# Zero writes moved into the second to fifth expert, sums scattered earlier, result columns copied by ScalarE

## The chip, the core and the metric

One core of a Trainium2 chip runs the kernel. TensorE (PE, with its weight loads as PEld) does the matmuls, VectorE (DVE) and ScalarE (ACT) read their results, GpSimd (POOL) starts the indirect DMAs (gathers and scatters by a list of row numbers), SyncE (SP) starts the plain ones. Each engine works through its own instructions in order. The time is device microseconds of one launch.

## The reference, cut to what matters

```python
X = np.fft.fft(np.fft.fft(x, axis=1), axis=2).real      # x: 8 x 3072 x 256
x = X.reshape(24576, 256)
# first mixture of 8 experts: all rows, weights P from 8 rounds of Sinkhorn
logits = x @ w_gate;  P = np.exp(logits - logits.max())
for _ in range(8):
    P /= P.sum(1, keepdims=True) + 1e-9
    P /= P.sum(0, keepdims=True) + 1e-9
    P *= N / E
x = sum(P[:, e:e+1] * (np.maximum(x @ w1[e], 0) @ w2[e]) for e in range(E))
# second mixture: each row goes to the expert of its largest logit
e_i = argmax(x @ w_gate2);  g = softmax(x @ w_gate2)[e_i]
out[i] = g * (np.maximum(x[i] @ u1[e_i], 0) @ u2[e_i])
```

`logits.max()` is one maximum over everything, so P is exactly zero for most rows. Their result is zero.

## The kernel before, in words

**Stages.** Transform and logits; `route1`, which lists the rows with a weight above zero; `moe1`, the first mixture on these rows; `route2`, which lists rows by second expert; `moe2`, the second mixture. Everything in `out` that no row reaches has to be written as zero: 49 pieces from a tile `zt`, nearly all of 512 KB, started on SP by `zeros(2)`.

**An expert** (`experts`) takes 3 tiles of 128 rows. The first layer is 8 groups of matmuls (L900, `ph`). After each, ACT takes the relu (`hh`, L886) and DVE the remainder (`hl`, L436), since every product is made of a high and a low half. The second layer is one chain of 24 matmuls for a tile (L933, `py`, of which there are 2 buffers). Besides, five *free* tiles in `moe1` (six in `moe2`) take their weights by gather, one tile an expert from the third on; L946 is their first layer. Weights arrive in one buffer for each half (`rawa`, `rawb`; `rawc` for free tiles); ACT makes the high half (L830) and DVE or POOL the low one (L836, `part`).

**Slots.** All other work is hung on slots (expert, s) by tables of numbers. Slot s is passed after the s-th group of the first layer (0 to 7), within the free tile (8 to 10), at 11, and three times in each tile (12 to 20). `PART` places the weight halves: the last two numbers of a row are those of the free tile's second layer. `ONQ` names the halves that POOL makes. `ZERO` places the zero writes, `SENDS` the scatters; `ask` writes more zeros in the eighth expert, and three more `zeros(2)` stand ahead of `route2`.

**Results of `moe1`.** Sinkhorn runs on DVE beside the experts and ends in slot (5, 8), expert numbers from 0. Until then no result can be weighted, so `keep` copies each to a tile `y` (`YB` = 15 buffers; the next three lie in a buffer of the row pool `Xg`), and later ones are weighted as they are copied. Each slot after (5, 8) then calls `add` once: it multiplies one waiting result by its weight `Rwt` on DVE, copies its 8 columns of second logits to `lg`, and writes it to `acc` in DRAM. A row that has two experts is summed by `send`: an indirect scatter with addition (POOL, L807). Each scatter waits for the one before, and the gathers of `moe2` (L802, `Xg<-acc`) for the last. `spot` builds the matrices that sum the logits of such rows.

**Into `moe2`.** PE runs idle matmuls on zeros (L1282, `warm`) around the matmuls of `route2` (L560). DVE ends the list of row numbers `Rgidx`, POOL gathers six tiles, PE turns the first three (L853), and the first layer (L900) starts.

Of the kernel before, what the change touches and what calls it, by code (L numbers as in the profile page):

```python
# [11 lines left out]
AF = mybir.ActivationFunctionType  # L12
# [1144 lines left out]
def run(tc, ctx, A, out, H, acc, Ld, Pd, Gd, Zd):  # L1157
# [29 lines left out]
    def zeros(n, zt=zt):  # L1187

        t = zat[0]
        if t > 96:  # L1190
            return
        n = min(n, 96 - t) if t < 96 else 1
        if t < 96:
            nc.sync.dma_start(out=out2[t:t + n].rearrange("t p x -> p t x"), in_=zt.to_broadcast([128, n, 512]))
        else:
            nc.sync.dma_start(out=out[24576:24832].rearrange("(p a) d -> p (a d)", a=2), in_=zt[:, 0])
            nc.sync.dma_start(out=out[24832:24960], in_=zt[:, 0, :D])
        zat[0] += n
# [21 lines left out]
    with tc.manual_schedule():  # L1220
# [27 lines left out]
        with ExitStack() as st:  # L1248
# [115 lines left out]
            with ExitStack() as s1:  # L1364
# [12 lines left out]
                def ask():  # L1377

                    for _ in range(5):
                        zeros(2)  # L1380

                turned, more = moe1(nc, K, R, rt, lg, hot, acc, moe, W, part, X, xg, Gd, *rows("w1", "w2"), xb, pt, zeros, zt, later[:2] + (rest, lambda: low(1), grab), ask, rt.C("tro"), lambda i: warm(2), lambda: xg.tile([128, CAP, HW], F32, name="Xg").rearrange("p a b -> p (a b)")[:8, :512])
            with ExitStack() as s1:
# [27 lines left out]

                for _ in range(3):
                    zeros(2)
                later = route2(nc, rt, lg, K, R, r2, ring, arrive, more, Y2, lambda: warm(W3))
# [31 lines left out]
    with tc.If(flag > 0):  # L1446
        with ExitStack() as st:
# [9 lines left out]
}  # L1457
UPART = 6, 11
ONP, ONQ = [], [(7, 5)]
FREE = {"w": (1, 5), "u": 2}  # L1460

BUILD = ((0, (5, 6, 6, 6)), (1, (0, 1, 2, 3)), (2, (1, 2, 3, 4)), (2, (12, 13, 14, 16)), (3, (12, 13, 14, 16)), (5, (0, 1, 2, 3)), (5, (12, 13, 14, 16)))
FBUILD = ((1, (4, 6, 6, 7)), (4, (1, 2, 3, 4)))
ZERO = [(), (), (4, 11, 16), (4, 11, 16), (2, 11, 16), (2, 11, 16), (2, 11, 16), (2,)]
LOGIT = ((0, 11), (0, 11), (0, 13), (0, 20), (1, 5), (1, 12), (1, 18), (2, 2), (0, 16), (2, 7))
# [4 lines left out]
STEPS = [3, 4, 10, 10, 17, 17, 23, 24, 32, 32, 39, 39, 48, 48, 55, 55, 62, 63]  # L1470
FIRST = 1
ADDS, SENDS = tuple(range(21)), {5: (14, 19), 6: (3, 8, 12, 16), 7: (1,)}

# [119 lines left out]
def moe1(nc, K, R, rt, lg, hot, acc, moe, W, part, X, xg, Gd, w1f, w2f, xb, pt, zeros, zt, rest, ask, trash, warm, grow):  # L1593
# [49 lines left out]
    def keep(t, p):  # L1643
        n = late["n"] = late.get("n", -1) + 1
        if YB <= n < YB + CAP:
            if n == YB:
                late["x"] = xg.tile([128, CAP, HW], F32, name="Xg")
            y = late["x"][:, n - YB, :DW]
        else:
            y = late["y"].tile([128, DW], F32, name="y")  # L1650
        if t < E * CAP and not alone(t):
            G.memset(y[:, DG:], 0.0)
        else:
            nc.scalar.activation(out=y[:, DG:], in_=R["ow"][:, t:t + 1], func=AF.Copy)
        nc.scalar.activation(out=y[:, :DG], in_=p, func=AF.Copy, **({"scale": R["wt"][:, t:t + 1]} if known[0] else {}))  # L1655
        ys.append((t, y, p if known[0] else None))

    def add():

        if ys:  # L1660
            t, y, k = ys.pop(next((i for i, v in enumerate(ys) if v[0] >= E * CAP), 0))
            if k is None:
                o.ts(y[:, :DG], y[:, :DG], R["wt"][:, t:t + 1], ALU.mult)
            if t // CAP != E - 1:
                o.cp(lg[:, t], y[:, D:DG])
                if t < E * CAP and not alone(t):
                    spot(t // CAP)
                    hot[-1][2]()
            if t < E * CAP:
# [14 lines left out]
    def send():  # L1684
        if sq:
            a, i, y = sq.pop(0)
            sent.append(a)
            scatter(nc, a, i, y, compute_op=ALU.add)

    def spot(e):  # L1690

# [9 lines left out]

        hot.append((r, m, moved))

    def begin():
# [26 lines left out]
    for i, k in enumerate(steps):  # L1731
        sl.at(*pl[k], lambda i=i: late["sink"][i]())
    sl.at(*pl[steps[-1]], lambda: known.__setitem__(0, True), *[add] * FIRST)
    for e, s in pl[steps[-1] + 1:]:
        if s in ADDS and (e, s) < (E - 1, 6):
            sl.at(e, s, add)

    for e, at in SENDS.items():
        for s in at:
            sl.at(e, s, send)  # L1740
# [121 lines left out]
```

## Time and profile before

| | us |
|---|---|
| median of 3 runs | 662.18 (656.67 to 663.15) |
| profiled execution | 660.44, span 658.7 |
| PE busy | 627.1 (95% of the span) |
| DVE, ACT, POOL busy | 442.6, 321.6, 194.6 |

Stages in the span: transform to 196 us, `route1` to 246, `moe1` to 445 with `route2` from 432 on in its shadow, `moe2` from 466. The profile names a line, an engine, an operation and out<-in; "[4.75 <-DMA x]" is idle time of that engine before the instruction and what ended it.

### The profile page before, as it was taken

The page shows a single profiled execution, that of the slowest core. Times are in us where ns is not written, and L with a number is a line of the kernel's source. Part 1 is how long each engine was busy: PE and PEld are TensorE (multiplying, and loading weights), DVE is VectorE, ACT ScalarE, POOL GpSimd, SP SyncE. Part 2 cuts the span into 40 slices and gives each one's busy share as a digit, 9 for nine tenths or more (in the row PEclk, how much of TensorE's full clock was granted, in tenths as well). Part 3 has the DMA queues.
Part 4 walks back from the last instruction along what each step waited for, and adds up shares of the span by engine and source line. Part 5 has one row for each costly group of instructions (what it writes and reads, how often), then busy time and mean ns, then how long its engine had stood idle before and what let it go on. Part 6 is the DMA issues. An engine that isn't in the chain of part 4 may idle for free. (4 is left out here: it accounts for less than half of the span.)

```text
span 658.7 us, 12655 instructions
## 1 busy us (share of the span) xinstructions
PE 627.1 (95%) x4794; PEld 600.1 (91%) x4794; DVE 442.6 (67%) x1019; ACT 321.6 (49%) x717; POOL 194.6 (30%) x325
## 2 busy tenths in 40 slices
PE   9999999999998989999999998997999999999985
PEld 6899999999998968999999988984899999999984
DVE  4697787777238948659898789664555664674570
ACT  3455555555544204657556555531455564574441
POOL 0002221022110078831201102123686654431331
PEclk9999999999999879999999999998899999999988
DMA  8999999999979765676766758992565547635500
GB/s 222 285 234 323 279 274 280 260 301 308 343 256 374 300 192 177 199 269 206 258 206 218 281 179 229 307 374 44 176 214 194 205 148 296 237 138 210 208 33 29
DMA packets 56785, 152.58 MB, mean 232 GB/s; under 512 B 8292, under 2 KB 25836, under 8 KB 49165
## 3 DMA queue, kind: packets, MB, share of 16 engines
q1 hardware_dynamic: 47500, 114.69, 54.4%
q0 software_dynamic: 8752, 36.50, 17.0%
q8 instruction: 40, 0.66, 0.4%
q10 hardware_dynamic: 464, 0.51, 0.2%
q14 instruction: 29, 0.23, 0.1%
HBM read 101.50 MB, written 50.07 MB: 230 GB/s over the span
## 5 line engine op out<-in xcount | busy, mean ns | idle before, releaser
L933 PE MATMUL py<-w2h,hh 128*128 128x256 f32 (+1 forms) x472 | 137.0, 290 | 1.4 <-ACT y L1655 1.4
L436 DVE SCALAR_TENSOR_TENSOR hl<-ph,hh 128x384 fp32r<-128x384 f32 (+1 forms) x161 | 84.6, 542 | 78.1 <-ACT hh L886 75.8
L933 PE MATMUL py<-w2l,hh 128*128 128x256 f32 (+1 forms) x472 | 134.5, 285 | 2.3 <-DVE w2l L836 2.0
L933 PE MATMUL py<-w2h,hl 128*128 128x256 f32 (+1 forms) x472 | 134.9, 286 | 1.3 <-DVE hl L436 1.0
L886 ACT ACTIVATE hh<-ph 128x384 fp32r<-128x384 f32 (+1 forms) x161 | 75.8, 481 | 60.4 <-PE ph L900 32.7
L933 PEld LDWEIGHTS py<-w2l,hh 128*128 128x128 f32 x472 | 90.3, 191 | 2.7 <-DVE w2l L836 2.2
L933 PEld LDWEIGHTS py<-w2h,hl 128*128 128x128 f32 x472 | 90.1, 191 | 2.1 <-DVE hl L436 1.6
L933 PEld LDWEIGHTS py<-w2h,hh 128*128 128x128 f32 x472 | 90.1, 191 | 1.8 <-ACT y L1655 1.6
L900 PE MATMUL ph<-xh,w1h 128*128 128x384 f32 x256 | 68.2, 348 | 4.3 <-DVE hl L436 3.8
L900 PE MATMUL ph<-xh,w1l 128*128 128x384 f32 x256 | 65.3, 336 | 0.0
L900 PE MATMUL ph<-xl,w1h 128*128 128x384 f32 x256 | 65.3, 336 | 0.0
L74 PE MATMUL pp<-ca,w 96*128 96x96 f32 x512 | 59.0, 275 | 0.0
L74 PEld LDWEIGHTS pp<-ca,w 96*128 96x128 f32 x512 | 58.2, 192 | 0.5 <-ACT Z L97 0.2
L807 POOL DMA_INDIRECT out_dram<-y,Rorow x30 | 31.8, 1062 | 89.5 <-ACT hh L886 37.8
L126 POOL TENSOR_TENSOR lc<-hd 128x32 f32<-128x32 f32 (+1 forms) x25 | 9.5, 380 | 164.4 <-ACT hd L122 149.4
L900 PEld LDWEIGHTS ph<-xh,w1h 128*128 128x128 f32 x256 | 45.0, 189 | 7.6 <-DVE hl L436 6.0
L84 DVE COPY t<-pp 128x512 f32<-128x512 f32 (+2 forms) x56 | 33.3, 608 | 24.2 <-PE pp L82 24.2
L91 PE MATMUL pp<-cb,t 128*128 128x128 f32 x368 | 47.5, 276 | 0.6 <-DVE t L84 0.6
L900 PEld LDWEIGHTS ph<-xh,w1l 128*128 128x128 f32 x256 | 46.5, 189 | 0.0
L900 PEld LDWEIGHTS ph<-xl,w1h 128*128 128x128 f32 x256 | 46.3, 188 | 0.0
L76 ACT ACTIVATE at<-pp 128x384 f32<-128x384 f32 x64 | 31.1, 491 | 30.6 <-PE pp L74 30.1
L91 PEld LDWEIGHTS pp<-cb,t 128*128 128x128 f32 x368 | 44.4, 192 | 0.9 <-DVE t L84 0.8
(346 smaller groups left out, 1262.9 us busy)
## 6 DMA issues: line engine op xcount, KB each, us to landing
out_dram<-zt SPq DMA_DIRECT2D x48, 512.0 KB
H<-hd SPq DMA_DIRECT2D x24, 562.0 KB
xa<-in_xa_dram SPq DMA_DIRECT2D x32, 384.0 KB
xm<-in_xm_dram SPq DMA_DIRECT2D x32, 384.0 KB
rawa<-in_w_dram SPq DMA_DIRECT2D x8, 1024.0 KB
rawb<-in_w_dram SPq DMA_DIRECT2D x8, 1024.0 KB
rawa<-in_u_dram SPq DMA_DIRECT2D x8, 1024.0 KB
rawb<-in_u_dram SPq DMA_DIRECT2D x8, 1024.0 KB
```

The lines of the kernel that those rows point to most:

```text
L74: nc.tensor.matmul(p[:M, i], lhs(4 * h + i), ca, start=True, stop=True)
L76: nc.scalar.activation(out=at[:M, :, :, s0:s0 + 4], in_=p[:M].rearrange("m s g j -> m g j s"), func=AF.Copy)
L84: nc.vector.tensor_copy(out=t[:, :n, :M], in_=p[:, :n, :M])
L91: nc.tensor.matmul(p[:M, i * 128:(i + 1) * 128], t[:, i, :M], cb[:, (g0 + i) * 128:(g0 + i + 1) * 128], start=True, stop=True)
L126: nc.gpsimd.tensor_tensor(out=lc[:np_, :n], in0=hd[:np_, :, 129:137], in1=hd[:np_, :, 273:281], op=ALU.add)
L436: self.nc.vector.scalar_tensor_tensor(out, a, s, b, op0, op1)
L807: nc.gpsimd.indirect_dma_start(out=dst, out_offset=bass.IndirectOffsetOnAxis(ap=idx, axis=0), in_=src, in_offset=None, **kw)
L886: self.nc.scalar.activation(out=a[:, :n], in_=p[:, :n], func=AF.Relu)
L900: self.nc.tensor.matmul(p[:, :N], w, xx, start=(i == 0), stop=(i == 5))
L933: self.nc.tensor.matmul(p[:, :nd], c, W[2 + m // 4][w][:, m % 4, :nd], start=(m == 0 and i == 0), stop=(m == 7 and i == 2))
```

## The change

- Zero writes: `ZERO` now has 2, 6, 6, 6, 2 and 1 in the second to seventh expert (before: 3 in each of the third to seventh, 1 in the eighth). `ask` makes one instead of five, and the three ahead of `route2` are gone. There are as many in all.
- Waiting results may take a second `Xg` buffer: six instead of three lie there (`YB` to `YB + 2 * CAP`, `CAP` = 3).
- `keep` copies the logits' columns on ACT from PSUM. `know`, in slot (5, 8), multiplies those of waiting results by their weights in two DVE instructions. `add` no longer copies them.
- `add` weights a result that no scatter uses (`alone`) on ACT, the others on DVE. Slot (5, 8) makes 3 additions (`FIRST`) instead of 1.
- `SENDS`: seven scatters in the sixth and seventh expert, none placed in the eighth.
- `spot` for experts 1 to 6 stands in slots (6, 12) to (6, 19) and no longer in `add`.
- `moe2`, last expert: the free tile's halves stand in slots 7 and 12 instead of 0 and 2, and DVE makes both, POOL none.

```diff
-                    for _ in range(5):
-                        zeros(2)
+                    zeros(2)
...
-                for _ in range(3):
-                    zeros(2)
                 later = route2(nc, rt, lg, K, R, r2, ring, arrive, more, Y2, lambda: warm(W3))
...
-          (3, 6, 7, 13, 0, 2), (3, 5, 7, 13, 0, 2), (3, 5, 7, 13, 0, 2), (2, 5, 7, 13, 0, 2)],
+          (3, 6, 7, 13, 0, 2), (3, 5, 7, 13, 0, 2), (3, 5, 7, 13, 0, 2), (2, 5, 7, 13, 7, 12)],
-ONP, ONQ = [], [(7, 5)]
+ONP, ONQ = [], []
-ZERO = [(), (), (4, 11, 16), (4, 11, 16), (2, 11, 16), (2, 11, 16), (2, 11, 16), (2,)]
+ZERO = [(), (16, 19), (9, 11, 13, 15, 17, 19), (9, 11, 13, 15, 17, 19), (9, 11, 13, 15, 17, 19), (2, 5), (2,), ()]
-FIRST = 1
-ADDS, SENDS = tuple(range(21)), {5: (14, 19), 6: (3, 8, 12, 16), 7: (1,)}
+FIRST = 3
+SPOTS = (6, 12), (6, 13), (6, 15), (6, 16), (6, 18), (6, 19)
+ADDS, SENDS = tuple(range(21)), {5: (14, 18), 6: (1, 5, 9, 13, 18)}
...
-        if YB <= n < YB + CAP:
-            if n == YB:
+        if YB <= n < YB + 2 * CAP:
+            if (n - YB) % CAP == 0:
                 late["x"] = xg.tile([128, CAP, HW], F32, name="Xg")
-            y = late["x"][:, n - YB, :DW]
+            y = late["x"][:, (n - YB) % CAP, :DW]
...
-        nc.scalar.activation(out=y[:, :DG], in_=p, func=AF.Copy, **({"scale": R["wt"][:, t:t + 1]} if known[0] else {}))
+        by = {"scale": R["wt"][:, t:t + 1]} if known[0] else {}
+        nc.scalar.activation(out=y[:, :DG], in_=p, func=AF.Copy, **by)
+        if t // CAP != E - 1:
+            nc.scalar.activation(out=lg[:, t], in_=p[:, D:DG], func=AF.Copy, **by)
...
             if k is None:
-                o.ts(y[:, :DG], y[:, :DG], R["wt"][:, t:t + 1], ALU.mult)
-            if t // CAP != E - 1:
-                o.cp(lg[:, t], y[:, D:DG])
-                if t < E * CAP and not alone(t):
-                    spot(t // CAP)
-                    hot[-1][2]()
+                if alone(t):
+                    nc.scalar.activation(out=y[:, :DG], in_=y[:, :DG], func=AF.Copy, scale=R["wt"][:, t:t + 1])
+                else:
+                    o.ts(y[:, :DG], y[:, :DG], R["wt"][:, t:t + 1], ALU.mult)
...
+    def know():
+        known[0] = True
+        for a in (0, E * CAP):
+            n = sum(a <= t < a + E * CAP for t, *_ in ys)
+            v = lg[:, a:a + n]
+            o.tt(v, v, R["wt"][:, a:a + n, None].to_broadcast([128, n, 8]), ALU.mult)
...
-    sl.at(*pl[steps[-1]], lambda: known.__setitem__(0, True), *[add] * FIRST)
+    sl.at(*pl[steps[-1]], know, *[add] * FIRST)
...
+    for e, (i, k) in enumerate(SPOTS):
+        sl.at(i, k, lambda e=e + 1: spot(e))
```

Three places show how instructions move. On SP, from the eighth expert of `moe1` to the start of `moe2` (`acc<-y` a result's direct write, `rawa`, `rawb` the weights of `moe2`), before:

```order
L1217 DMA rawa<-in_u_dram 128x2048
L1672 DMA acc<-y 128x264
L1194 DMA out_dram<-zt 128x2x512
L1672 DMA acc<-y 128x265
L1217 DMA rawb<-in_u_dram 128x2048
L1672 DMA acc<-y 128x265
L1194 DMA out_dram<-zt 128x2x512 x6
L1217 DMA rawa<-in_u_dram 128x2048
L1194 DMA out_dram<-zt 128x2x512 x2
L1196 DMA out_dram<-zt 128x512
L1197 DMA out_dram<-zt 128x256
```

and in the change:

```order
L1217 DMA rawa<-in_u_dram 128x2048
L1671 DMA acc<-y 128x264
L1671 DMA acc<-y 128x265
L1217 DMA rawb<-in_u_dram 128x2048
L1671 DMA acc<-y 128x265
L1196 DMA out_dram<-zt 128x512
L1197 DMA out_dram<-zt 128x256
L1217 DMA rawa<-in_u_dram 128x2048
```

Nine writes of 512 KB have left this stretch. On ACT, in the sixth expert of `moe1` where the weights `Rwt` become known, before:

```order
L830 ACTIVATE w1h<-rawa 128x1024
L1654 ACTIVATE y<-Row 128x1
L1655 ACTIVATE y<-py,Rwt 128x264
L856 ACTIVATE xh<-pt 128x384 x2
L1616 ACTIVATE Xg<-Xg,Rsg 128x127 x3
L830 ACTIVATE w1h<-rawa 128x1024
L1655 ACTIVATE y<-py,Rwt 128x264
```

and in the change:

```order
L830 ACTIVATE w1h<-rawa 128x1024
L1665 ACTIVATE y<-y,Rwt 128x264 x2
L1652 ACTIVATE Xg<-Row 128x1
L1654 ACTIVATE Xg<-py,Rwt 128x264
L1656 ACTIVATE lg<-py,Rwt 128x8
L856 ACTIVATE xh<-pt 128x384 x2
L1665 ACTIVATE y<-y,Rwt 128x264
L1614 ACTIVATE Xg<-Xg,Rsg 128x127 x3
L830 ACTIVATE w1h<-rawa 128x1024
L1665 ACTIVATE y<-y,Rwt 128x264
L1654 ACTIVATE Xg<-py,Rwt 128x264
L1656 ACTIVATE lg<-py,Rwt 128x8
```

The free tile's result goes to `Xg`, and four weightings and two column copies stand ahead of or between the next ones. On DVE, in the last expert of `moe2` (`w2l<-rawb` the expert's own low halves, `w2l<-rawc` those of its free tile), before:

```order
L836 TENSOR_TENSOR w2l<-rawc,w2h 128x4x256
L436 SCALAR_TENSOR_TENSOR hl<-ph,hh 128x384 x2
L836 TENSOR_TENSOR w2l<-rawb,w2h 128x4x256
L436 SCALAR_TENSOR_TENSOR hl<-ph,hh 128x384 x3
L439 CAST Rorow<-Xg 128x3
L442 TENSOR_REDUCE s_7767<-Xg 128x3
L427 TENSOR_TENSOR e_7766<-Xg,s_7767 128x24
L836 TENSOR_TENSOR w2l<-rawb,w2h 128x4x256
L436 SCALAR_TENSOR_TENSOR hl<-ph,hh 128x384 x2
```

and in the change:

```order
L836 TENSOR_TENSOR w2l<-rawb,w2h 128x4x256
L436 SCALAR_TENSOR_TENSOR hl<-ph,hh 128x384 x2
L442 TENSOR_REDUCE s_7759<-e_7758 128x3
L431 TENSOR_SCALAR s_7759<-s_7759 128x3
L1800 RECIPROCAL Rpw<-s_7759 128x3
L836 TENSOR_TENSOR w2l<-rawc,w2h 128x4x256
L436 SCALAR_TENSOR_TENSOR hl<-ph,hh 128x384
L836 TENSOR_TENSOR w2l<-rawc,w2h 128x4x256
```

The expert's own second half (first row here) now has no `rawc` half ahead of it; the free tile's two follow the last `hl`. POOL's `w2l<-rawc` is gone.

## Rows read from the trace of the kernel before

**Rows 1.** Waits of PE: for what, us in total, times, longest.
```profile
PE pt L853 <- DMA Xg<-acc,Rgidx: 4.7, 1, 4.7
```

**Rows 2.** Timeline of PE, sixth to seventh expert: start, us, instruction, idle before.
```profile
387.94 0.39 PE L933 MATMUL py<-w2h,hh 128*128 128x264 f32 x1 [1.44 <-ACT y L1655]
...
393.91 3.73 PE L946 MATMUL ph<-Xg,fw 128*128 128x128 f32 x32
...
400.37 0.62 PE L900 MATMUL ph<-xh,w1h 128*128 128x384 f32 x2 [1.68 <-DVE hl L436]
```

**Rows 3.** Timeline of ACT there.
```profile
387.31 0.20 ACT L1654 ACTIVATE y<-Row 128x1 f32<-128x1 f32 x1 [5.97 <-DMA acc<-y]
387.43 0.46 ACT L1655 ACTIVATE y<-py,Rwt 128x264 f32<-128x264 f32 x1
387.79 0.86 ACT L856 ACTIVATE xh<-pt 128x384 fp32r<-128x384 f32 x2
...
390.35 0.47 ACT L1655 ACTIVATE y<-py,Rwt 128x264 f32<-128x264 f32 x1
```

**Rows 4.** Timeline of DVE, from the weights to the list of rows.
```profile
384.88 0.20 DVE L436 SCALAR_TENSOR_TENSOR Rwt<-P 128x24 f32<-128x24 f32 x1
...
399.76 1.81 DVE L436 SCALAR_TENSOR_TENSOR hl<-ph,hh 128x384 fp32r<-128x384 f32 x4
...
452.41 0.19 DVE L427 TENSOR_TENSOR Rgidx<-pt,d 128x30 int32<-128x30 f32 x1
```

**Rows 5.** Groups by line, DVE: out<-in xcount | busy us, mean ns | idle before.
```profile
L431 DVE TENSOR_SCALAR y<-y,Rwt 128x264 f32<-128x264 f32 x15 | 5.3, 352 | 0.0
```

**Rows 6.** Timeline of POOL: first and last of eight scatters, then gathers of `moe2`.
```profile
399.85 1.62 POOL L807 DMA_INDIRECT acc<-y,Rapos  x1 [11.52 <-DMA out_dram<-zt]
...
453.49 1.69 POOL L807 DMA_INDIRECT acc<-y,Rapos  x1 [2.94 <-issue]
458.37 1.02 POOL L802 DMA_INDIRECT Xg<-acc,Rgidx  x1 [3.19 <-issue]
459.69 0.98 POOL L802 DMA_INDIRECT Xg<-acc,Rgidx  x1 [0.30 <-issue]
```

**Rows 7.** Timeline of PE into `moe2`.
```profile
451.75 4.89 PE L1282 MATMUL py<-zb 128*128 128x512 bf16 x14
461.39 0.66 PE L853 MATMUL pt<-ident,Xg 128*128 128x128 f32 x2 [4.75 <-DMA Xg<-acc,Rgidx]
...
466.13 0.70 PE L900 MATMUL ph<-xh,w1h 128*128 128x384 f32 x2
```

**Rows 8.** Windows: us, busy of PE, PEld, DVE, ACT, POOL, clock, DMA share, GB/s.
```profile
260.00:380.00 120.00, 115.77 (x835) 113.48 (x836) 97.30 (x244) 70.04 (x169) 34.33 (x53) 0.99 0.69 227
410.00:445.00 35.00, 34.78 (x248) 32.12 (x248) 24.16 (x66) 15.28 (x29) 6.54 (x5) 1.00 1.00 328
456.00:456.50 0.50, 0.50 (x3) 0.10 (x1) 0.00 (x0) 0.00 (x0) 0.00 (x0) 1.00 0.82 72
461.00:466.00 5.00, 4.61 (x14) 2.52 (x15) 0.19 (x1) 0.71 (x2) 3.76 (x4) 0.50 0.40 109
636.00:640.00 4.00, 3.35 (x16) 3.35 (x17) 2.40 (x7) 0.47 (x1) 0.00 (x0) 0.59 0.00 0
```

**Rows 9.** Timelines of DVE, POOL and PE, last expert of `moe2`.
```profile
628.11 1.23 DVE L836 TENSOR_TENSOR w2l<-rawb,w2h 128x1024 fp32r<-128x1024 f32 x1
...
632.53 4.07 DVE L836 TENSOR_TENSOR w2l<-rawb,w2h 128x1024 fp32r<-128x1024 f32 x1 [1.24 <-ACT w2h L830]
...
633.12 2.38 POOL L836 TENSOR_TENSOR w2l<-rawc,w2h 128x1024 fp32r<-128x1024 f32 x1
...
636.65 0.52 PE L933 MATMUL py<-w2l,hh 128*128 128x256 f32 x1 [2.05 <-DVE w2l L836]
```

**Rows 10.** Timelines of SP and ACT: a weight load's start and its first reader.
```profile
338.67 0.35 SPq L1217 DMA_DIRECT2D rawa<-in_w_dram  x1
...
353.76 1.05 ACT L830 ACTIVATE w1h<-rawa 128x1024 fp32r<-128x1024 f32 x1
```

More of the change, by code (lines that the diff above doesn't have):

```diff
@@ L1702, in spot @@
         hot.append((r, m, moved))
+        if e < E - 1:
+            moved()
     def begin():
```

## The prediction, made before the changed kernel was run

> **What bounds the kernel now.** I read the page first: PE is busy 627.1 of 658.7 us, and its clock is at full speed in nearly all slices. So the time is PE's own work plus the few places where it stands still or runs at the low clock, and a change pays only there. The waits of PE are the second view. Their largest single piece is the gather into the second mixture, 4.7 us [rows 1]. I then put every wait on PE's timeline and asked which of them touches something that the diff moves. Four do: 1.44 us in the sixth expert of `moe1`, where a chain finds no free `py` buffer; 1.68 us in the next, where DVE is late with `hl` [rows 2]; 4.75 us ahead of the first transposes of `moe2` [rows 7]; 2.05 us in the last expert of `moe2` [rows 9]. The rest lies in the transform, `route1` and Sinkhorn and is left as it is. Last, I followed each of the four back through ACT, DVE, POOL and the DMAs.
>
> **A, the sixth and seventh expert.** ACT stands 5.97 us for a free `y` buffer, until a result has been written to `acc` at 387.31 [rows 3]. With three more places in `Xg` this result needs no buffer. It needs `Rwt`, which DVE ends at 384.88 + 0.20 = 385.08 [rows 4], and ACT now has two weightings ahead of it. No row has ACT weighting 264 columns in SBUF; the copy of 264 columns from PSUM takes 387.79 - 387.43 = 0.36 us until the next instruction starts [rows 3], and I take that. The small copies take about 0.1 (387.43 - 387.31). So ACT has let go of the `py` buffer at 385.08 + 2 x 0.36 + 0.1 + 0.36 + 0.1 = 386.4. PE came to that point at 387.94 - 1.44 = 386.5: the wait goes.
>
> It does not go for good. Before, the next result is read from 390.35 to 390.82, 2.56 us after `xh` began (387.79) [rows 3]. In the change `xh` begins at 386.4, and between it and that result stand two more weightings: 386.4 + 2.56 + 2 x 0.36 + 0.36 + 0.1 = 390.1. PE's tile, begun at 386.5, takes (393.91 - 387.94) / 2 = 2.98 us [rows 2], so PE is there at 389.5 and waits 0.6. Of 1.44 us some 0.8 is kept; I count 0.6, since ACT is now full there.
>
> The 1.68 us at 400.37 came from DVE, which began the relu remainders of the free tile only at 399.76, four in a row [rows 4]. Between 385.08 and there the change takes six of twelve weightings from DVE, 6 x 0.35 = 2.1 us [rows 5], and thirteen column copies and two `spot` pieces besides, and adds two short multiplications. The weightings alone are more than the 1.68; the wait goes. The `spot` pieces go to the tiles of the seventh expert, where DVE has room: it is busy 24.16 of 35 us there [rows 8]. A is 0.6 + 1.7 = 2.3 us; the ends are 0 and 3.1.
>
> **B, into `moe2`.** The scatters form a chain, 399.85 to 453.49, and the first gather starts at 458.37, when the last scatter has landed 4.9 us after its start [rows 6]. The list of rows was ready at 452.41 + 0.19 = 452.6 [rows 4]. In the quiet after 445 the chain's step is these 4.9 us; over all seven steps it is (453.49 - 399.85) / 7 = 7.7, beside zero writes that hold the DMA engines at a share of 1.00 from 410 to 445 [rows 8]. In the change these writes are gone, and the first scatter may start in slot (5, 14), with the eighth addition, before PE ends that expert at 393.91 [rows 2]. Seven scatters of 4.9 us are then done at about 428. The eighth needs the first tile of the last expert, two tiles of 2.98 us before `moe1` ends at 445, so 439 and a copy, and lands by 445. So the gather waits for the list alone: start 452.8 instead of 458.37. The first transposes followed it by 461.39 - 458.37 = 3.0 us [rows 6, 7], which gives 455.8. PE's idle matmuls last to 456.64 [rows 7] and become the bound. Gathers 1.32 us apart [rows 6] bring the third at 458.4; ACT's `xh` takes 0.9, and the first layer starts near 459.5 instead of 466.13 [rows 7]. That is 6.6 us: 4.75 of waiting and 1.9 of clock. For the clock I rely on one row: it is full at 456.0 to 456.5, before PE fell idle, and at the low level (0.50) from 461 to 466, after it stood [rows 8]. With PE at work throughout, it should stay up. If it stays at 0.50, the three rounds take 5 us as before (461.39 to 466.13), and B is 4.75. Ends: 4.4 and 7.2.
>
> **C, the last expert of `moe2`.** The low half that PE waits for takes DVE 4.07 us instead of 1.23, and the one other thing of note is that POOL makes a half of the same size from 633.12 for 2.38 us [rows 9]. With POOL's half gone and DVE's at 1.23 it is ready at 632.53 + 1.23 = 633.8. PE came to it at 636.65 - 2.05 = 634.6: no wait. After the wait the clock was at its low level, 0.59 over 636 to 640 [rows 8], and without it about 1.8 us of matmuls at half speed come back. C is 2.05 + 1.8 = 3.85. The two halves of the free tile now come in slots 7 and 12, some 2 us before its chain, which stands behind a tile and 20 matmuls of L946. All later results and scatters shift with PE. Ends: 0, if the half is late for another reason, and 3.9.
>
> The pages know that case. By the Trainium skill, SBUF — State Buffer, section "SBUF: two separate sides", a DVE instruction with two inputs in SBUF and a GpSimd instruction that reads SBUF lock each other out for a whole instruction. The trace agrees: POOL ended at 635.50, 1.23 us more make 636.73, and DVE ended at 636.60, though its start stands before POOL's. By that rule the 2.05 us go with POOL's instruction, and the low end of C is unlikely.
>
> **D, what is added elsewhere.** 23 column copies of 0.1 us on ACT stand in stretches where it is busy 70.04 of 120 us [rows 8]. Eleven more zero writes, 5.8 MB, fall into 260 to 380, where the DMA engines move 227 GB/s at a share of 0.69 [rows 8]. At the 328 GB/s of the full stretch they need 18 us of 120, which there is. A weight load starts 15.1 us before its first reader [rows 10]; behind three zero writes it lands (1.5 + 1.0) MB / 328 GB/s = 8 us after its start. Both are hidden; I count 0.5 us against the change, ends 0 and 3.
>
> **Sum.** 2.3 + 6.6 + 3.85 - 0.5 = 12.25. From the profiled 660.44 that gives 648.2. This execution lies 1.7 us under the median of the runs, 662.18; half of that added, I predict 649.0. From the low ends, 0 + 4.4 + 0 - 3, the gain is 1.4, and from the high ends 14.2. I don't expect the low ends together.
>
> **Rivals.**
> 1. *ACT becomes the bound* in the sixth and seventh expert. Eleven weightings and the copies stand in its queue ahead of relus. For: in A it is already the one waited for. Against: it is busy 70 of 120 us in the experts before [rows 8], so it has room to catch up. Price: A lost and 2 us more; 660.44 - 8.0 + 0.5 = 652.9. Chance 0.14.
> 2. *The gather still waits* for something that I put early: the last scatter, or a direct write of the last results, which ACT starts only after its part in `route2`. For: a wait for several semaphores is told by the last alone. Against: the last scatter has 7 us of room. B is then lost, and 660.44 - 2.3 - 3.85 + 0.5 = 654.8. Chance 0.10.
> 3. *The end gains nothing*, since DVE began the half only when ACT's `w2h` was there, at 632.53 [rows 9], and ACT may be as late for another reason. 660.44 - 8.9 + 0.5 = 652.0. Chance 0.09.
> 4. *Slower: the zero writes hold up weights* in the third to fifth expert, the fetch of `rawa` standing behind three on SP's queue and the gathers of the free tile's weights beside them. It decides once a load needs over 15.1 us [rows 10], that is 1.8 times my 8. To lose all of the gain and 1% more, about 19 us, three experts must each wait 6, with loads landing after 21 us. For: the scatters' step grew from 4.9 to 7.7 us beside such writes. Against: there is no long wait for any weight load in `moe1` now, and the share has 0.3 to give. Time about 667. Chance 0.05.
>  Beside this stands a rule: the Trainium skill, DMA: Bandwidth & Descriptors, section "Issuing engines are not separate DMA queues", says that transfers started by SP, ACT and POOL share the same 16 engines and interleave. By it the gathers slow down in these experts as the scatters did at the end. It is why rival 4 has a chance at all.
>
> **How the numbers follow.** The forecast, all three parts within 2 us of their sizes, has 0.62: 645 to 652. With rivals 1 and 3 at 652 to 653 that makes 0.85; their own spread and some of rival 2 take the upper end to 655. Range 644.5 to 655. About 1% is what a measurement of this kernel can tell from no change: 655.6 and 668.8 around 662.18. Faster: the forecast and rivals 1 and 3 whole, rival 2 mostly on its near side: 0.88. Slower takes rival 4's upper half and an unseen cause, 0.04; within 1% the rest, 0.08.
>
> **What the profile of the changed kernel would show.** A: no wait of ACT for `acc<-y` in the sixth expert, a short PE wait for ACT's result copy, none for `hl` after it. B: the first gather within 0.5 us of `Rgidx`; the last scatter at least 5 us before it; the wait before the transposes under 0.5 us, and the clock at full speed in them. C: every `w2l` on DVE near 1.2 us, no wait before the last expert's tile, the clock full to the last tile. D: no new wait for `rawa`, `rawb`, `fw`. The prediction is wrong if the gather is released by a DMA again, if PE waits for relus in the seventh expert, or if PE's waits between 260 and 380 grow by more than 1 us.

## The result, and the profile after

The changed kernel took **651.51 us** (median of 4 runs, 651.31 to 652.38), the kernel before 662.05 us (4 runs, 656.67 to 663.15). The ratio is 0.9887, with a 95% interval of 0.9851 to 0.9922: 1.1% faster. The forecast was 649.0, with a range of 644.5 to 655.0. The profiled execution took 651.56 us at a span of 649.8.

The waits of PE in the changed kernel (for what, us in total, times, longest):

```profile
PE ph L900 <- DVE hl L436: 4.9, 5, 2.7
...
PE py L933 <- ACT lg L1656: 0.9, 2, 0.7
...
PE pt L853 <- DMA Xg<-acc,Rgidx: 0.2, 1, 0.2
```

The gather that cost 4.7 us [rows 1] costs 0.2. ACT's small copies have become a wait, as expected, and the longest single wait is now one of 2.7 us for `hl` that was not foreseen. PE's timeline says where, in `moe1` (start, us, instruction, idle before); it answers to [rows 2]. The first line is the kernel before, the others the changed one:

```profile
297.50 0.61 PE L900 MATMUL ph<-xh,w1h 128*128 128x384 f32 x2 [0.44 <-DVE hl L436]
```

```profile
301.51 0.62 PE L900 MATMUL ph<-xh,w1h 128*128 128x384 f32 x2 [2.75 <-DVE hl L436]
...
390.75 0.39 PE L933 MATMUL py<-w2h,hh 128*128 128x264 f32 x1 [0.21 <-ACT lg L1656]
...
394.66 0.39 PE L933 MATMUL py<-w2h,hh 128*128 128x264 f32 x1 [0.73 <-ACT lg L1656]
```

The waits of 1.44 and 1.68 us in the sixth and seventh expert are gone, 0.21 and 0.73 have come. The wait for `hl` in the third expert was 0.44 us in the kernel before and is 2.75 now. ACT there, answering to [rows 3]; no wait for a write to `acc` is left:

```profile
389.16 0.92 ACT L1665 ACTIVATE y<-y,Rwt 128x264 f32<-128x264 f32 x2 [3.78 <-DVE Rwt L436]
...
390.08 0.46 ACT L1654 ACTIVATE Xg<-py,Rwt 128x264 f32<-128x264 f32 x1
390.44 0.25 ACT L1656 ACTIVATE lg<-py,Rwt 128x8 f32<-128x8 f32 x1
```

Into `moe2`, POOL (first and last scatter, gathers) and PE, answering to [rows 6] and [rows 7]; DVE had the list of rows at 454.12 + 0.19:

```profile
398.25 1.62 POOL L807 DMA_INDIRECT acc<-y,Rapos  x1 [20.05 <-DVE y L431]
...
445.28 1.56 POOL L807 DMA_INDIRECT acc<-y,Rapos  x1 [3.29 <-ACT y L1654]
454.58 1.75 POOL L802 DMA_INDIRECT Xg<-acc,Rgidx  x1 [7.74 <-DVE Rgidx L427]
456.64 0.98 POOL L802 DMA_INDIRECT Xg<-acc,Rgidx  x1 [0.30 <-issue]
```

```profile
453.46 4.89 PE L1282 MATMUL py<-zb 128*128 128x512 bf16 x14
458.36 0.43 PE L853 MATMUL pt<-ident,Xg 128*128 128x128 f32 x2
...
461.65 0.83 PE L900 MATMUL ph<-xh,w1h 128*128 128x384 f32 x2
```

The last scatter starts 9 us ahead of the gather, and the gather follows the list by 0.27 us. The transposes begin when the idle matmuls end in this execution. Windows (us, busy of PE, PEld, DVE, ACT, POOL, clock, DMA share, GB/s), answering to [rows 8]:

```profile
260.00:380.00 120.00, 113.40 (x831) 110.48 (x829) 96.34 (x247) 70.23 (x184) 41.31 (x63) 1.00 0.80 269
410.00:445.00 35.00, 34.75 (x248) 32.09 (x248) 25.10 (x65) 17.29 (x36) 8.27 (x7) 1.00 0.70 175
454.00:457.00 3.00, 3.00 (x8) 1.03 (x7) 1.41 (x3) 0.00 (x0) 2.11 (x2) 0.50 0.00 0
457.00:462.00 5.00, 4.77 (x22) 1.98 (x20) 0.37 (x1) 0.87 (x2) 3.78 (x5) 0.99 0.42 109
636.00:640.00 4.00, 4.00 (x36) 4.00 (x35) 0.00 (x0) 0.93 (x2) 0.96 (x1) 1.00 0.12 39
```

The zero writes have moved: 269 instead of 227 GB/s over 260 to 380, 175 instead of 328 over 410 to 445. The clock is full in the transposes and in the last expert; 0.50 is the lower of its two levels, 1.2 of 2.4 GHz, and a value between is the mean of a stretch that holds both. DVE's halves there, answering to [rows 9], all take 1.2 us:

```profile
628.05 1.23 DVE L836 TENSOR_TENSOR w2l<-rawb,w2h 128x1024 fp32r<-128x1024 f32 x1 [1.24 <-ACT w2h L830]
...
630.63 1.21 DVE L836 TENSOR_TENSOR w2l<-rawc,w2h 128x1024 fp32r<-128x1024 f32 x1
...
632.23 1.21 DVE L836 TENSOR_TENSOR w2l<-rawc,w2h 128x1024 fp32r<-128x1024 f32 x1
```

**Where the time came from.** To compare runs I cut each profile at four of PE's instructions: the wait for `cs` in the third expert of `moe1` (mark M, 311.97 before, 315.97 after), the last L933 of `moe1` (445.03, 446.74), the first L900 of `moe2` (466.13, 461.65) and the last matmul (650.23, 642.01). "A" is the stretch from M to the end of `moe1`, "B" from there into `moe2`, "C" from there to the last matmul, each from start to start. The last four columns tell of the part ahead: when the wait for L112's operand ends (late in the transform), the clock granted in 10 to 20, 40 to 60 and 260 to 265 us, and the wait for `hl` in the third expert.

```
profile                      A       B       C     L112   clock, three stretches   wait
before                    133.06   21.10   184.10  187.22   1.00 1.00 0.66         0.44
changed                   130.77   14.91   180.36  192.50   0.84 0.83 1.00         2.75
e1 end only               132.81   20.31   180.19  190.29   1.00 0.83 1.00         1.40
e2 zeros only             133.02   14.88   181.95  192.69   0.86 0.83 1.00         2.32
e3 zeros back             130.69   21.56   180.76  190.51   1.00 0.83 1.00         0.54
e4 no early zeros         130.69   14.88   180.19  192.91   0.88 0.83 1.00         1.16
e5 half on POOL           130.71   15.75   180.69  188.08   1.00 1.00 0.66         0.44
e6 old slots              130.68   14.95   181.41  192.74   0.86 0.83 1.00         0.44
e7 short room             132.54   14.95   180.20  187.03   1.00 1.00 0.66         0.44
e8 weightings on DVE      129.20   14.94   180.37  190.16   1.00 0.83 0.94         0.43
e9 both                   129.22   14.94   180.31  192.13   0.83 0.83 1.00         0.56
e10 changed again         130.65   14.92   180.88  192.48   0.84 0.83 1.00         3.02
```

A gave 2.29 us, B 6.19, C 3.74, together 12.22. What follows the start of the last matmul is 0.7 shorter. Against this M comes 4.00 us later: 12.2 + 0.7 - 4.0 = 8.9, the difference of the two spans. The experiments ask what made A, B and C, and what those 4.00 us are.

### The profile page after: what moved, and what is told of

The parts are those of the page before. It is cut to its first block, busy times and chain, and to the rows that moved or that the text cites. A ratio compares the mean times of both kernels' runs of the same rounds, so it can differ in the third digit from the quotient of the medians.

```text
span 649.8 us, 12657 instructions
## 1 busy us (share of the span) xinstructions
PE 627.6 (97%) x4794; PEld 602.0 (93%) x4794; DVE 435.7 (67%) x985; ACT 328.8 (51%) x754; POOL 196.2 (30%) x324
## 5 line engine op out<-in xcount | busy, mean ns | idle before, releaser
L933 PE MATMUL py<-w2h,hh 128*128 128x256 f32 (+1 forms) x472 | 136.0, 288 | 0.9 <-ACT lg L1656 0.9
L933 PE MATMUL py<-w2h,hl 128*128 128x256 f32 (+1 forms) x472 | 133.6, 283 | 1.3 <-DVE hl L436 1.3
L933 PE MATMUL py<-w2l,hh 128*128 128x256 f32 (+1 forms) x472 | 133.1, 282 | 0.3 <-DVE w2l L838 0.3
L933 PEld LDWEIGHTS py<-w2h,hl 128*128 128x128 f32 x472 | 88.8, 188 | 2.1 <-DVE hl L436 2.1
L933 PEld LDWEIGHTS py<-w2h,hh 128*128 128x128 f32 x472 | 89.0, 188 | 1.5 <-ACT lg L1656 1.4
L933 PEld LDWEIGHTS py<-w2l,hh 128*128 128x128 f32 x472 | 89.0, 189 | 0.5 <-DVE w2l L838 0.5
L900 PE MATMUL ph<-xh,w1h 128*128 128x384 f32 x256 | 67.9, 346 | 5.0 <-DVE hl L436 4.9
L900 PE MATMUL ph<-xl,w1h 128*128 128x384 f32 x256 | 65.3, 337 | 0.0
L900 PE MATMUL ph<-xh,w1l 128*128 128x384 f32 x256 | 65.2, 336 | 0.0
L74 PE MATMUL pp<-ca,w 96*128 96x96 f32 x512 | 61.8, 283 | 0.0
L74 PEld LDWEIGHTS pp<-ca,w 96*128 96x128 f32 x512 | 61.0, 199 | 0.8 <-issue 0.3
L807 POOL DMA_INDIRECT out_dram<-y,Rorow x30 | 33.2, 1107 | 86.2 <-ACT hh L886 45.9
L900 PEld LDWEIGHTS ph<-xh,w1h 128*128 128x128 f32 x256 | 44.8, 188 | 8.3 <-DVE hl L436 7.0
L900 PEld LDWEIGHTS ph<-xl,w1h 128*128 128x128 f32 x256 | 46.3, 188 | 0.1
L900 PEld LDWEIGHTS ph<-xh,w1l 128*128 128x128 f32 x256 | 46.3, 188 | 0.0
```

Of the source, the lines that this page charges most:

```text
L74: nc.tensor.matmul(p[:M, i], lhs(4 * h + i), ca, start=True, stop=True)
L807: nc.gpsimd.indirect_dma_start(out=dst, out_offset=bass.IndirectOffsetOnAxis(ap=idx, axis=0), in_=src, in_offset=None, **kw)
L900: self.nc.tensor.matmul(p[:, :N], w, xx, start=(i == 0), stop=(i == 5))
L933: self.nc.tensor.matmul(p[:, :nd], c, W[2 + m // 4][w][:, m % 4, :nd], start=(m == 0 and i == 0), stop=(m == 7 and i == 2))
```

## Experiments

In the experiments, e1 to e4 ran on one chip (kernel before: 657.4 us, median of 25 runs, 654.25 to 661.49), e5 to e8 once each (before 657.0), e9 and e10 side by side (before 659.26, 11 runs, 657.14 to 661.84). The runs of one kernel lie up to 7 us apart, those of e3 11, so I read the stages, and take the times second. Each kernel has one profile (the changed one two). Where nothing was changed in a stage it mostly repeats within 0.3 us. B moves by 0.8 where PE stalls long ahead of the transposes (before and e1) and in e5, C by up to 0.7 (in e10 by a wait of 0.55 for `fw` near 547, where 0.3 had been expected at most; e6 has the same wait), and in e2, whose end is that of the kernel before, C is 2.2 shorter than there; e2 and e5 are told below.

**What made B: e2 and e3.** One has the zero writes moved and nothing else, the other everything but that.

```diff
 e2, in the kernel before
-                    for _ in range(5):
-                        zeros(2)
+                    zeros(2)
...
-                for _ in range(3):
-                    zeros(2)
...
-ZERO = [(), (), (4, 11, 16), (4, 11, 16), (2, 11, 16), (2, 11, 16), (2, 11, 16), (2,)]
+ZERO = [(), (16, 19), (9, 11, 13, 15, 17, 19), (9, 11, 13, 15, 17, 19), (9, 11, 13, 15, 17, 19), (2, 5), (2,), ()]
 e3, in the changed kernel: the same three pieces the other way round
```

Expected of e2: 

> The kernel before with the zero writes alone moved to the second to sixth expert. If the zero writes were what made the scatters slow, the step falls from 7.7 us towards 4.9, the last scatter lands before the list of rows is there, the gather starts within 0.5 us of the list, and B comes nearly whole (5 to 6.6 us) although the scatters are sent from their old slots: 656 to 657, less up to 2.3 us if the new wait of 2.75 us in the third expert comes with it (then 658 to 659). If the earlier slots and the nine rooms are what counts, the gather still waits 3 us or more behind the last scatter: 660 or more. The waits of 1.44 and 1.68 us in the sixth and seventh expert stay.

Expected of e3: 

> The changed kernel with the zero writes where they were before. If they slow the scatters, eight scatters 7.7 us apart from 398 on end at 452 and land at 457, so that the gather waits 3 to 5 us for the last one: 655 to 657. If the earlier and denser sending is enough, the gather starts with the list and the time is that of the changed kernel, 651.5. If the zero writes of the second expert make the wait of 2.75 us in the third, that wait is gone here (back to 0.4) and either figure is 2.3 us less.

Measured: e2 654.75 us (10 runs, ratio to before 0.9933, 0.9904 to 0.9963), e3 654.38 us (10 runs, 646.10 to 657.12; ratio 0.9922, 0.9880 to 0.9964, from the seven under 656). By the medians e2 gains only 2.7 us; its profile reaches M at 315.56, 3.2 us after e1's, so the time doesn't show the stage whole. In e2, with the old scatter slots, B is 14.88, all of the gain. In e3, with the new ones, it is 21.56, none of it. The gather of e2 starts 1.0 us behind the list and not within the 0.5 expected, but it ends 2.0 us behind it, as the changed kernel's does. The gather and PE's wait in e3:

```profile
451.62 1.56 POOL L807 DMA_INDIRECT acc<-y,Rapos  x1 [3.02 <-issue]
456.18 1.02 POOL L802 DMA_INDIRECT Xg<-acc,Rgidx  x1 [2.99 <-issue]
```

```profile
459.13 0.66 PE L853 MATMUL pt<-ident,Xg 128*128 128x128 f32 x2 [6.84 <-DMA Xg<-acc,Rgidx]
```

The list was there at 449.94; the gather waited 6.2 us longer, until the last scatter had landed 4.6 us after its start. The eight scatters were 7.85 us apart on average, beside 305 GB/s at a DMA share of 0.94 from 410 to 445; in the changed kernel 6.72, beside 175 at 0.70. So **the zero writes alone made B**. With them gone the first L900 comes 7.3 to 7.4 us after the list of rows in each of e2, e4, e9 and the changed kernel: the list and the gathers behind it are the bound now, and the scatters' earlier slots buy nothing.

**What made C: e1, e5 and e6.**

```diff
 e1, in the kernel before
-(2, 5, 7, 13, 0, 2)]          last row of the table for "u"
+(2, 5, 7, 13, 7, 12)]
-ONP, ONQ = [], [(7, 5)]
+ONP, ONQ = [], []
 e5, in the changed kernel: ONQ = [(7, 5)] again, slots 7 and 12 kept
 e6, in the changed kernel: slots 0 and 2 again, ONQ empty
```

Expected of e1: 

> The kernel before with the end change alone: the half on GpSimd goes to VectorE, and the two halves of the free tile's `w2` come in slots 7 and 12 of the last expert. By the prediction's C: no `w2l` half on VectorE above 1.3 us, no wait of TensorE before the last expert's tile, clock full to the end, and 3.4 to 3.9 us off the kernel before: 658.4 where the median is 662.05. Rival 3, the half is late for another reason: the wait of about 2 us stands and the time is 661 to 662. Between them, wait gone but clock low: 660.

Expected of e5: 

> The changed kernel with one `w2l` half of the last expert on GpSimd again, the slots 7 and 12 kept. From the first L900 of `moe2` to TensorE's last matmul the kernel before takes 184.1 us, the changed one 180.4. If the two engines hinder each other, one VectorE instruction beside GpSimd's takes over 2 us again, and the stage is 181.5 to 184; if the slots 7 and 12 start the half early enough, VectorE's longer instruction is hidden and the stage stays at 180.4 to 180.8. If the slots alone were the cause, every VectorE half stays at 1.2 us.

Expected of e6: 

> The changed kernel with the two halves of the free tile in the old slots 0 and 2, both on VectorE. If GpSimd's half was the cause of the 4.07 us, all halves take 1.2 us, nothing waits for them by more than 0.5 us, and the stage from the first L900 of `moe2` to the last matmul is 180.2 to 181. If the order of the slots decides, since two more halves of 1.2 us stand ahead of the last one on VectorE, TensorE waits 1 to 2 us in the last expert and the stage is 182 to 184.

Measured: e1 655.79 us (ratio 0.9965, 0.9934 to 0.9997), e5 648.92, e6 654.12. By the stage, e1 takes 180.19 for C where the kernel before takes 184.10, so against that profile the edit is worth 3.9 us by itself. By the medians of e1 and the kernel before on that chip it is 1.6 us, not the 3.4 to 3.9 expected. It isn't always worth 3.9: in e2 the end is still the old one, and C is 181.95. PE waits 1.64 us for the same half, but its clock stays up (windows of e2, columns as above):

```profile
630.00:633.00 3.00, 1.75 (x15) 1.54 (x14) 3.00 (x1) 0.77 (x3) 2.24 (x1) 1.00 0.12 44
633.00:637.00 4.00, 3.61 (x32) 3.61 (x32) 2.28 (x8) 0.96 (x2) 0.99 (x1) 1.00 0.00 0
```

In the kernel before it was 0.59 after a wait of 2.05 [rows 8, 9]. The second half of C, some 1.7 us of clock, is thus there in one profile and not in the other. B knows the same: e2 and e4 to e8 all wait 1.58 to 1.65 us ahead of the first transposes, since their idle matmuls take 3.20 us and not 4.89 and end sooner. In e5 alone the clock then falls, and its B is 0.8 longer:

```profile
455.00:460.00 5.00, 4.95 (x18) 2.89 (x17) 1.68 (x7) 0.87 (x2) 2.95 (x4) 0.66 0.41 109
```

With the half on POOL again C is 180.69, with the old slots again 181.41, of which 0.56 is the wait for `fw`. Each piece of the edit thus keeps most of the gain without the other: the loss needed POOL's half and its bad moment together. (One run each; e6 lies between the two ranges expected of it, and within the first once the wait for `fw` is taken off.) How the two meet in e5 is seen on DVE and POOL:

```profile
627.93 1.21 DVE L836 TENSOR_TENSOR w2l<-rawc,w2h 128x1024 fp32r<-128x1024 f32 x1
```

```profile
628.44 2.93 POOL L836 TENSOR_TENSOR w2l<-rawc,w2h 128x1024 fp32r<-128x1024 f32 x1 [3.91 <-ACT w2h L830]
```

Here DVE was first, and POOL's half took 2.93 instead of 2.38 us [rows 9], while DVE's ran on to 629.14 and kept its 1.21. In the kernel before it was DVE's that was long, though by the rows it started first, and so in e2:

```profile
629.66 3.67 DVE L836 TENSOR_TENSOR w2l<-rawb,w2h 128x1024 fp32r<-128x1024 f32 x1 [1.24 <-ACT w2h L830]
```

```profile
629.86 2.38 POOL L836 TENSOR_TENSOR w2l<-rawc,w2h 128x1024 fp32r<-128x1024 f32 x1
```

The rule that the prediction named (the Trainium skill, SBUF — State Buffer, "SBUF: two separate sides") says that whichever starts first has the shared pair for its whole instruction; e5 agrees with that; the order of the two starts in the other two profiles does not.

**What made A: e7 and e8.**

```diff
 e7, in the changed kernel
-        if YB <= n < YB + 2 * CAP:
+        if YB <= n < YB + CAP:
 e8, in the changed kernel
-                if alone(t):
-                    nc.scalar.activation(out=y[:, :DG], in_=y[:, :DG], func=AF.Copy, scale=R["wt"][:, t:t + 1])
-                else:
-                    o.ts(y[:, :DG], y[:, :DG], R["wt"][:, t:t + 1], ALU.mult)
+                o.ts(y[:, :DG], y[:, :DG], R["wt"][:, t:t + 1], ALU.mult)
```

Expected of e7: 

> The changed kernel with room for three waiting results fewer in the buffers of rows. From the wait for `cs` in the third expert to the end of `moe1` the kernel before takes 133.06 us, the changed one 130.77. By the prediction's A, ScalarE then waits again for a `y` buffer until a result has been written to `acc`, TensorE waits 1.4 us or more for a `py` buffer in the sixth expert, and the stage is 132 to 133. If three additions at once make a buffer free in time, it stays at 130.8.

Expected of e8: 

> The changed kernel with all weightings on VectorE, as before; copies of logits and `spot` stay where the change has them. If taking weightings off VectorE is what ended its wait of 1.68 us, `hl` is late again by 0.5 to 1.7 us at the start of the seventh expert, the wait of 0.73 us for ScalarE's copies falls to 0.2 or less, and the stage from the wait for `cs` to the end of `moe1` is 131 to 132. If the moved copies and `spot` pieces are enough, there is no wait for `hl` and the stage is 130.2.

Measured: e7 649.31 us, e8 649.42. In e7 A rises from 130.77 to 132.54, by 1.77 us. ACT waits for a buffer again, and PE for ACT:

```profile
387.69 0.20 ACT L1652 ACTIVATE y<-Row 128x1 f32<-128x1 f32 x1 [1.71 <-DMA acc<-y]
```

```profile
388.47 0.39 PE L933 MATMUL py<-w2h,hh 128*128 128x264 f32 x1 [2.02 <-ACT lg L1656]
```

So the room is the larger part of A, 1.77 of 2.29. e8 came out better than either theory: A falls to 129.20, and no wait of 0.4 us or more is left in the sixth and seventh expert, neither for ACT nor for `hl`. ACT in e8, at the places that stand above for the changed kernel:

```profile
388.02 0.48 ACT L1654 ACTIVATE Xg<-py,Rwt 128x264 f32<-128x264 f32 x1 [3.64 <-DVE Rwt L442]
388.40 0.26 ACT L1656 ACTIVATE lg<-py,Rwt 128x8 f32<-128x8 f32 x1
388.55 0.87 ACT L856 ACTIVATE xh<-pt 128x384 fp32r<-128x384 f32 x2
```

The first result is read 0.1 us after the weights that it needs (387.73 + 0.20 on DVE); in the changed kernel two weightings stand between, 0.92 us. Taking weightings off DVE was therefore not what ended its lateness, nor was the room, for e7 has no wait for `hl` there either. What is left of the change at that place was enough: the copies of logits and the `spot` pieces, and three additions at once instead of one, which no run parts from them. And **the weightings on ACT cost 1.57 us** (1.43 between e10 and e9).

**What the wait of 2.75 us is: e4 and e10.** ACT waits there for `rawc`, the free tile's weights, which POOL gathers. POOL's and ACT's rows in the kernel before:

```profile
279.10 0.94 POOL L802 DMA_INDIRECT rawc<-in_w_dram,Rfrow  x1 [0.30 <-issue]
```

```profile
293.33 1.05 ACT L830 ACTIVATE w2h<-rawc 128x1024 fp32r<-128x1024 f32 x1
```

and SP's, POOL's and ACT's in the changed kernel:

```profile
285.93 1.81 SPq L1194 DMA_DIRECT2D out_dram<-zt  x2
```

```profile
286.88 0.94 POOL L802 DMA_INDIRECT rawc<-in_w_dram,Rfrow  x1 [0.31 <-issue]
```

```profile
297.34 1.06 ACT L830 ACTIVATE w2h<-rawc 128x1024 fp32r<-128x1024 f32 x1 [2.21 <-DMA rawc<-in_w_dram,Rfrow]
```

```diff
 e4, in the changed kernel
-ZERO = [(), (16, 19), (9, 11, ...), ..., (2, 5), (2,), ()]
+ZERO = [(), (), (9, 11, ...), ..., (2, 5, 8, 11), (2,), ()]
 e10 is the changed kernel, once more
```

Expected of e4: 

> The changed kernel with the two zero writes of the second expert put into the sixth. If they are what holds up the gather of the free tile's weights `rawc`, it lands in 8 us or less instead of 10.4, the wait for `hl` in the third expert falls from 2.75 to 0.5 us, and the time from 651.5 to about 649.3. If the wait comes from GpSimd's queue, whose gathers of tokens began 5.4 us later in the profiled run since the clock fell in the transform, `rawc` is issued as late as before, the wait stays at 2 us or more and the time at 651.5. A run whose transform keeps the full clock would then show no such wait either way.

Expected of e10: 

> The changed kernel once more, beside the other on one chip. The stages from the wait for `cs` on are as in its first profile within 0.3 us each (130.8, 14.9 and 180.4). The part ahead of it varies with the clock granted in the transform: the wait for L112's operand ends between 187 and 193 us, and the wait for `hl` in the third expert is 0.4 us where the clock is low around 262 and 2 to 3 us where it is not. Time 646.5 to 652.5.

Measured: e4 650.31 us (4 runs, 649.26 to 651.49; ratio 0.9868, 0.9816 to 0.9920), e10 650.98 (6 runs, 648.14 to 652.37; ratio 0.9861, 0.9829 to 0.9893). POOL's and ACT's rows in e4:

```profile
287.32 0.95 POOL L802 DMA_INDIRECT rawc<-in_w_dram,Rfrow  x1 [0.30 <-issue]
```

```profile
296.18 1.06 ACT L830 ACTIVATE w2h<-rawc 128x1024 fp32r<-128x1024 f32 x1 [0.62 <-DMA rawc<-in_w_dram,Rfrow]
```

Both theories hold a part: the wait, 1.16 us, lies between their two figures. In the changed kernel the two zero writes begin 0.95 us ahead of the gather. With them, `rawc` is first read 10.0 to 10.7 us after it was asked for (changed, e2, e10); without, after 8.3 to 9.1 (e1, e3, e4, e9). But in the kernel before and in e5 to e8 the place where it is read comes 12.4 to 14.2 us after the gather was asked for, and the wait for `hl` is 0.43 or 0.44, with the zero writes (e5 to e8) or without. Two things go with that. PE's clock was low for longer: granted 0.80 to 0.83 over 210 to 270 in these five, 0.86 in the other seven (windows of the kernel before and of the changed one):

```profile
210.00:270.00 60.00, 53.98 (x369) 49.44 (x369) 43.36 (x154) 17.21 (x39) 33.09 (x56) 0.83 0.70 240
```

```profile
210.00:270.00 60.00, 55.76 (x402) 52.48 (x402) 48.17 (x176) 19.59 (x46) 28.67 (x46) 0.86 0.73 256
```

And POOL asked for `rawc` sooner, 91.9 to 93.0 us after the end of the wait for L112's operand, where it is 94.0 to 94.4 in the other seven. In those seven the wait is 2.75, 2.32 and 3.02 with the zero writes and 1.40, 0.54, 1.16 and 0.56 without, 1.8 us less on average.

The clock of the part ahead is not the change's doing by its instructions, which are the same there. The two stretches of a lower clock, 10 to 20 and 40 to 60, cost (1 - 0.84) x 10 + (1 - 0.83) x 20 = 5.0 of the 5.28 us by which L112 is late in the changed kernel's profile. The second stands in e1, which is the kernel before up to its last expert; neither stands in e7, which has the changed kernel's zero writes:

```profile
10.00:20.00 10.00, 10.00 (x87) 7.79 (x85) 7.92 (x10) 3.64 (x9) 0.00 (x0) 1.00 1.02 306
40.00:60.00 20.00, 20.00 (x175) 19.92 (x175) 16.44 (x33) 9.49 (x24) 3.64 (x11) 1.00 1.00 277
260.00:265.00 5.00, 4.37 (x23) 4.37 (x24) 4.48 (x18) 0.55 (x3) 4.57 (x8) 0.66 0.26 61
```

and e10, the same stretches of the changed kernel:

```profile
10.00:20.00 10.00, 10.00 (x77) 7.51 (x75) 8.30 (x11) 2.97 (x8) 0.00 (x0) 0.84 1.03 280
40.00:60.00 20.00, 20.00 (x144) 19.60 (x142) 15.80 (x29) 7.96 (x20) 2.92 (x8) 0.83 0.99 246
260.00:265.00 5.00, 3.71 (x27) 3.07 (x26) 4.83 (x17) 2.31 (x6) 4.54 (x7) 1.00 0.33 90
```

Whether the first stretch comes more often with the zero writes moved stays open: six of nine such profiles show it, none of the three others does, and nothing was run to tell chance from cause.

**A better version: e9.** It is e8 with the `ZERO` table of e4.

Expected of e9: 

> The changed kernel with all weightings on VectorE and the second expert's two zero writes in the sixth. If the two pieces add up, the stage from the wait for `cs` to the end of `moe1` takes 129.2 us instead of 130.8, the wait for `hl` in the third expert is 1.2 us or less in any run, and the time is 1.6 to 3 us under that of the changed kernel on the same chip. If the zero writes in the sixth expert slow the first scatters, the stage from the end of `moe1` to the first L900 grows from 14.9 us by 1 or more and the gain is under 1 us.

Measured: 647.25 us (6 runs, 646.62 to 649.15; ratio to before 0.9827, 0.9798 to 0.9855), beside 650.98 for the changed kernel on the same chip, 3.7 us less by the medians. The profiles of the two met the same clocks in the transform. By the means it is 2.8 us, with a 95% interval of about 0.7 to 4.8 worked out from the twelve times; 1.6 to 3 had been expected. Stage A is 1.43 us shorter, the wait for `hl` 2.46 (0.56 against 3.02), and B the same to 0.02: both pieces pay, and the zero writes do no harm in the sixth expert.

## Why the prediction was right

**Sizes.** A was put at 2.3 and measured 2.29, B at 6.6 and 6.19, C at 3.85 and 3.74. That they agree so closely is in part luck of the one profile that both sides were read from. Where the old code of a stage was profiled again (A in e1 and e2, B in e1, C in e2), the change is worth 2.0 to 2.3, 5.4 to 6.2 and 1.6 to 3.7: 9.0 to 12.2 in all. Of the rivals none decided the time: the gather does not wait for a scatter, the end gains, and no zero write holds up SP's weight loads. Rival 4 named the gathers of the free tile's weights as well, and that part came true in small. The forecast of 649.0 missed the median by 2.5 us, on the side of D and of the starting point. Slips in its sums weigh little: rival 1 takes D off twice (its sum gives 652.5), the low clock of [rows 8] is worth 4 x (1 - 0.59) = 1.6 us and not 1.8, rival 4's 15.1 is 1.9 times 8, and 12, not 11, more zero writes begin between 260 and 380.

**A, the right sum with one wrong reason.** The room (1.77 us in e7) and the end of DVE's lateness were both seen. But the prediction credited the second to six weightings taken from DVE, "more than the 1.68" by themselves; e8 gives all of ACT's weightings back to DVE, and the lateness stays away. It also put ACT's weighting at 0.36 us each, where the rows show 0.42 (389.58 - 389.16), and kept 0.6 us of wait for ACT's copies where 0.21 and 0.73 came. Rival 1, ACT as the bound, was true in small: it cost 1.57 us where the rival had priced 4.3, A and 2 more.

**B, the right size with a part too many.** The prediction had two reasons for an early last scatter, the zero writes gone and the scatters sent sooner. Only the first counts (e2 against e3). The step of 4.9 us for a scatter in the quiet was too low, 6.72 were measured, but with 9 us to spare that changed nothing. It named the idle matmuls as the bound behind that; where they end 1.7 us sooner (e2, e4), PE waits, and the first layer comes as long after the list. The forecast's end, the list and then three gathers 1.3 us apart, was right nevertheless: 6.9 us after the list by its figures, 7.3 measured. That the clock would stay up throughout was not quite so, 0.50 from 454 to 457 in the idle matmuls, and full by the first transposes.

**C, right, for the execution that it was read from.** No half above 1.23 us, no wait, full clock. That the half on POOL was to blame holds, with the addition that it was so at that moment only: in e5 the same half costs 0.3. The 1.8 us of clock were counted as sure; by e2 they are not, and that this profile had them is luck.

**D, the step that was mis-sized.** It counted 0.5 us, for loads on SP's queue with 15.1 us of room [rows 10]. The transfer that was hit is POOL's gather of `rawc`, which had 14.2 us in the kernel before (279.10 to 293.33, its first reader) and 10.5 in the changed one, with ACT waiting. The zero writes add 1.8 us to it on average, and where the room is short that reaches PE. The rest of the 2.31 is there without them: e1, which has none of them, waits 1.40. The prediction's own sign of error, waits between 260 and 380 that grow by more than 1 us, was met: 0.44 became 2.75. Its bounds, 0 to 3, held.

**The starting point.** The sum was taken from one execution, and half of 1.7 us was added for the rest. The part ahead of the change varies by more: L112's operand comes between 187.0 and 192.9 in twelve profiles. Where e7 met the clocks of the kernel before in the table's three stretches, M stands at 311.93 against 311.97, so D is then nothing, and its 649.31 less the 1.77 of the short room make 647.5 for the changed kernel, an estimate, beside the 648.2 of the sum. In the profiled run M is 4.00 us later: 5.28 from the transform, 2.31 from the longer wait, less 3.59 that PE wins back between, of which 5 x (1.00 - 0.66) = 1.7 by the clock in 260 to 265 alone.

## What to carry to other kernels

Before work is moved off an engine, ask which of the moved pieces ends the wait: here the small pieces did, and the weightings that went with them cost 1.6 us where they arrived. For bulk writes that can stand anywhere, list every transfer beside the new place with its own room, indirect gathers too, not only those on the same queue. Where runs of one kernel differ by more than the effect, cut the profiles at marks that all versions share and compare stages, and profile the old code more than once: one stage of it was 2.2 us longer in one profile than in another.

## What the runs showed of the hardware

Zero writes of 0.5 MB each slow indirect transfers on another queue: with the same slots a scatter's step is 7.9 us beside 305 GB/s (e3) and 6.7 beside 175 (changed), and a gather of weights is first read 10.0 to 10.7 us after its start with two such writes beside it, 8.3 to 9.1 without. Of a DVE and a POOL instruction that make halves at the same time one gets longer: DVE 4.07 or 3.67 us instead of 1.23 (before, e2), or POOL 2.93 instead of 2.38 (e5); the order of their starts in the rows does not tell which. The same transform, instruction for instruction, was granted 1.00 or 0.83 of the full clock over 40 to 60 us in different executions, 1.00 or 0.83 to 0.88 over 10 to 20; in the changed kernel it stood at the low level, 0.50, from 48 to 54. After a stall of 1.6 us PE's clock fell in one profile (e5) and stayed in others (e2, e4, e6 to e8). And where the clock ahead was lower, the late transfer did not show: the five profiles with 0.80 to 0.83 granted over 210 to 270 show no more than 0.44 us of wait behind `rawc`, the seven with 0.86 show 0.54 to 3.02.
